# Two token-mixing items queued behind the last attention's products with v, and w_out converted beside the last channel mixing

## The chip, the cores and the metric

The kernel runs on one core of a Trainium2 chip. Its engines are called TensorE (PE in the rows, PEld for its weight loads), VectorE (DVE), ScalarE (ACT), GpSimd (POOL) and SyncE (SP, which here issues every DMA). The metric is the device time of one launch in microseconds; the time before is the median of three runs.

## What is computed

```python
def _attn_ref(q, k, v):                       # 4 batches, 8 heads, 576 tokens, 64 features a head
    scores = scale * q @ k^T                  # heads 0-3: a window of 32 keys; heads 4-7: every 4th of 128
    return softmax(masked scores) @ v
def _moe_ref(x, w_theta, w_tok_r, w_tok_i, w_ch):
    theta = x @ w_theta
    zr = x * cos(theta);  zi = x * sin(theta)
    u = x + w_tok_r @ zr + w_tok_i @ zi       # token mixing, over 576 tokens
    return u + max(u @ w_ch, 0)               # channel mixing, 512 x 512
def _moe2_ref(x, w_in, w_spatial, b_spatial, w_out):
    h = max(x @ w_in, 0);  u, v = halves of h # 512 features each
    v_n = layer norm of v
    return (u * (w_spatial @ v_n + b_spatial)) @ w_out
```

The three functions follow one another for each of four batches. All products are made in fp32 accuracy by splitting both operands into a high and a low part and adding three products (high-high, low-high, high-low). Some weights arrive as 64-bit floats and are converted on the chip.

## The kernel before, in words

**Attention** of batch b is 12 groups (four pairs of heads, three groups g each), numbered 12b to 12b+11. A group makes scores, then two steps later transposes, then two steps after that products with v (`att_values`; g = 0 makes none, g = 1 makes 24 products for it and g = 0, g = 2 makes 12). ScalarE copies the result ps_x to x. The last two groups of batch 3 are 46 and 47.

**Theta** (`th_unit`) takes 128 tokens: VectorE makes a high and a low part of x (xh, xl, two buffers each), TensorE makes 12 products ps_th and four transposes of x, ScalarE and VectorE make sine and cosine, and VectorE and GpSimd make z in two parts (zh, zl). A unit t covers tokens 128t to 128t+127; the last 64 tokens of batches 2 and 3 share one unit (`th_shared`), which needs both batches' x. `th_keep` saves batch 2's part of it in xs.

**Token mixing** (`tm_run`) has eight items for a batch: two halves of the tokens times four stripes of 128 features. With K_MAIN an item is 8 x 3 products that add up in one tile ps_y of PSUM; VectorE adds it to x. The ninth part, k = 8, comes from the shared theta unit and is mixed later as items of its own for batch 2, three products each, which also split x into uh and ul.

**Channel mixing** (`ch_run`) has eight items ps_r of 12 products; each result is split into `parts` and stored to x2d in DRAM.

**Weights for the second half** (w_in, w_sp, w_out) are converted by the 32 jobs of `second` and stored to DRAM from two buffers `parts`, which channel mixing of batches 0 to 2 uses too. A job of w_out loads 64-bit words into a tile w64 (four buffers), shifts them on ScalarE (L128) and VectorE (L131 to L133), rounds them to the high part on ScalarE (L107) and subtracts for the low part on GpSimd (L144). Staging tiles come from a tag `stage` with four buffers, which `w_half` also uses; `w_half` is the first thing beside the last channel mixing.

**The second half** runs in pairs of batches: `hv_unit` (five a pair's first batch, four the second's), `hu_run`, `sp_run` (spatial gating; its last operands are vhl and vhb) and `out_unit`, each with tiles from `ps_2`.

**Order.** `spread` traces a main generator and, at given rates, fills beside it. A planner then sets each engine's queue from a simulated timeline, in which an instruction that is ready may go ahead of earlier ones that are not; tiles of one tag are handed out in the order of the program. The queue of each engine is then fixed and in order. PSUM has eight banks: `ps_mm` four (attention's scores, theta, mixing), `ps_t` three, `ps_v` one (c64, the scratch of the conversion).

Of the kernel before, what the change touches and what calls it, by code (L numbers as in the profile page):

```python
# [11 lines left out]
F32 = mybir.dt.float32  # L12
# [6 lines left out]
PSUM = bass.MemoryType.PSUM  # L19
# [4 lines left out]
P = 128  # L24
# [4 lines left out]
T = 64  # L29
KW = T + WIN  # L30
NT = S // T
NA = 6
# [12 lines left out]
ATT_RATE, ATT_RATE_PAIR = 2.0, 3.0  # L45
TAIL_RATE = 1.0
CH_BEFORE = 4
PE_MASK = 1
PAIR = 2


IN_ENG, SP_ENG, OUT_ENG = "vgg", "ag", "aga"
# [5 lines left out]
K_MAIN = (0, 4, 1, 5, 2, 6, 3, 7)  # L58
# [4 lines left out]
def tile_block(ctx: ExitStack, tc: tile.TileContext, qT, kT, vw, eye_in, mask_in, eye_b_in, w_theta, w_tok, w_ch, w_in, w_sp, w_sph, b_sp, w_out, out):  # L63
    nc = tc.nc
    V, A, G, PE, SY = nc.vector, nc.scalar, nc.gpsimd, nc.tensor, nc.sync
# [6 lines left out]
    ps_mm = ctx.enter_context(tc.tile_pool(name="ps_mm", bufs=4, space=PSUM))  # L72
# [23 lines left out]
    wth_h = pth.tile([P, 4, DM], F32R, name="wth_h")  # L96
    wth_l = pth.tile([P, 4, DM], F32R, name="wth_l")
    patt = tc.alloc_tile_pool(name="patt", bufs=2, side="right")
    ps_t = tc.alloc_tile_pool(name="ps_t", bufs=3, space=PSUM)

    ps_v = tc.alloc_tile_pool(name="ps_v", bufs=1, space=PSUM)
    c64 = ps_v.tile([P, 512], F32, name="c64")


    def copy(dst, src, eng):
# [85 lines left out]
    groups = [(b, hp, g) for b in range(B) for hp in range(4) for g in range(3)]  # L191
    att = {}
    heads = {}

    def att_load(b, hp):
        early = b == 0 and hp >= 2
# [73 lines left out]
    def att_values(m):  # L270

        b, hp, g = groups[m]
        if g == 0:
            return
        qz, kt, vt, pT = heads[b, hp]
        ps = ps_t.tile([P, 512], F32, tag="pt", name="ps_x")
        if g == 1:
            for t in range(NA):
                for j in range(2):
                    PE.matmul(ps[T * j:T * (j + 1), T * t:T * (t + 1)], vt[:, t, T * j:T * (j + 1)], pT[j][:, T * t:T * (t + 1)], start=True, stop=True)  # L280
        else:
            for t in range(NB):
                for j in range(2):
                    PE.matmul(ps[T * j:T * (j + 1), T * t:T * (t + 1)], vt[:, NA + t, T * j:T * (j + 1)], pT[2][:, P * t + T * j:P * t + T * (j + 1)], start=True, stop=True)
        n0, n1 = (0, NA * T) if g == 1 else (NA * T, S)
        if hp < 2:
            A.copy(x[b][:, hp, n0:n1], ps[:, :n1 - n0])
            return

        xv = x[b][:, hp, :].rearrange("p (i r) -> p r i", r=4)  # L290
        if g == 1:
            A.copy(xv[:, :2, :], ps[:, :2 * SEQ].rearrange("p (r i) -> p r i", r=2))
            A.copy(xv[:, 2, :NA * T - 2 * SEQ], ps[:, 2 * SEQ:NA * T])
        else:
            A.copy(xv[:, 2, NA * T - 2 * SEQ:], ps[:, :3 * SEQ - NA * T])
            A.copy(xv[:, 3, :], ps[:, 3 * SEQ - NA * T:NB * T])

    def attention(b):

        n0, n1 = 12 * b, 12 * (b + 1)  # L300
        for m in range(n0, n1 + LAG_V):
            if n0 <= m - LAG_V < n1:
                att_values(m - LAG_V)
            if n0 <= m - LAG_T < n1:
                att_transpose(m - LAG_T)
            if m < n1:
                att_scores(m)
            yield
# [65 lines left out]
    def th_shared(b):  # L374
        th_unit(b, 4, True)
        yield

    def th_run(b, ts):
        for t in ts:
            th_unit(b, t)  # L380
            yield
# [58 lines left out]
    def run(gen):  # L440
        for _ in gen:
            pass

    def spread(main, *fills):

        acc = [0.0] * len(fills)
        for _ in main:
            for i, (gen, rate) in enumerate(fills):
                acc[i] += rate
                while acc[i] >= 1.0:  # L450
                    acc[i] -= 1.0
                    next(gen, None)
        for gen, _ in fills:
            run(gen)

    def jobs(fns):
        for f in fns:
            f()
            yield

    def take(gen, n):
        for _ in range(n):
            yield next(gen)

    def chain(*gens):
        for g in gens:
            yield from g
# [11 lines left out]
    second = jobs(j_in + j_sp + j_out)  # L479
# [9 lines left out]
    spread(th_run(0, (4, 0, 1, 2, 3)), (jobs([lambda f=f: behind(f) for f in j_tok0]), 2.0))  # L489
    for b in range(PAIR):  # L490
        ch = ch_run(b)
# [3 lines left out]


    th_keep(PAIR)
    spread(tm_run(PAIR, K_MAIN, False), (chain(attention(PAIR + 1), th_shared(PAIR)), ATT_RATE_PAIR), (take(second, 10), 1.25))
    spread(th_run(PAIR + 1, (0, 1, 2, 3)), (chain(tm_run(PAIR, (8,)), ch_run(PAIR)), TAIL_RATE), (second, 2.5))
    patt.release()  # L500
    ps_v.release()
    ps_t.release()
    pth.release()

# [58 lines left out]
    def w3():  # L563
        if w3_jobs:
            w3_jobs.pop(0)()

    for _ in ch_run(3):
        w3()
    p1.release()

    p2 = tc.alloc_tile_pool(name="p2", bufs=1, side="left", reuse_waits="tile")
    ps_2 = tc.alloc_tile_pool(name="ps_2", bufs=4, space=PSUM)

    wo_h = p2.tile([P, 4, DM], F32R, name="wo_h")
    wo_l = p2.tile([P, 4, DM], F32R, name="wo_l")
# [1 line left out]
        SY.dma_start(f32(t), f32(wo_d[:, :, i]))  # L577

    def mmtile(name):
        return ps_2.tile([P, 512], F32, tag="m2", name=name)  # L580

    vh, vl, vhl = {}, {}, {}
    hu = {}
# [126 lines left out]
    for pr in (0, 2):  # L710
# [20 lines left out]
        out_unit(b0, 4)  # L731
        out_unit(b1, 3, 2 if pr else 1)
    ps_2.release()
    p2.release()
    p2s.release()
    p2r.release()
# [59 lines left out]
```

## Time and profile before

| | |
|---|---|
| median of three runs (lowest to highest) | 570.19 us (569.38 to 571.11) |
| the profiled execution, its span | 569.31 us, 567.5 us |
| mean granted clock of TensorE | 0.982 |
| busy: TensorE, its weight loads | 534.8 us (94%), 478.4 us (84%) |
| busy: VectorE, ScalarE, GpSimd | 331.0 us (58%), 241.9 us (43%), 262.1 us (46%) |
| moved by DMA | 76.07 MB, 134 GB/s over the span |

The span is the time from the first to the last instruction of the profiled execution. Matmuls are pipelined: their durations overlap, so the pace is read from the distance of their starts. A granted clock of 1.00 is 2.4 GHz, 0.50 is 1.2 GHz. All positions in the rows are microseconds from the start of the span.

### The profile page before, as it was taken

The page shows a single profiled execution, that of the slowest core. Times are in us where ns is not written, and L with a number is a line of the kernel's source. Part 1 is how long each engine was busy: PE and PEld are TensorE (multiplying, and loading weights), DVE is VectorE, ACT ScalarE, POOL GpSimd, SP SyncE. Part 2 cuts the span into 40 slices and gives each one's busy share as a digit, 9 for nine tenths or more (in the row PEclk, how much of TensorE's full clock was granted, in tenths as well). Part 3 has the DMA queues.
Part 4 walks back from the last instruction along what each step waited for, and adds up shares of the span by engine and source line. Part 5 has one row for each costly group of instructions (what it writes and reads, how often), then busy time and mean ns, then how long its engine had stood idle before and what let it go on. Part 6 is the DMA issues. An engine that isn't in the chain of part 4 may idle for free.

```text
span 567.5 us, 11263 instructions
## 1 busy us (share of the span) xinstructions
PE 534.8 (94%) x4148; PEld 478.4 (84%) x4148; DVE 331.0 (58%) x844; ACT 241.9 (43%) x710; POOL 262.1 (46%) x333
## 2 busy tenths in 40 slices
PE   5887689999999999998899999999999999999997
PEld 3665578888988999877888999899899889988996
DVE  3589899898797269747697115773610327354030
ACT  3766476635655435766444212432322224223222
POOL 3484687552995348944349534334211203332040
PEclk9979799999999999999799999999999999999999
DMA  8845636672259453667400799705025110001002
GB/s 213 221 129 171 162 112 181 196 216 82 74 176 263 138 163 106 206 208 233 144 8 33 264 362 381 242 3 167 0 75 164 42 55 1 1 1 68 8 1 94
DMA packets 49935, 76.07 MB, mean 134 GB/s; under 512 B 4052, under 2 KB 30552, under 8 KB 49880
## 3 DMA queue, kind: packets, MB, share of 16 engines
q1 hardware_dynamic: 49880, 75.35, 43.3%
q8 instruction: 33, 0.54, 0.4%
q14 instruction: 22, 0.18, 0.1%
HBM read 52.53 MB, written 22.81 MB: 133 GB/s over the span
## 4 chain that ended last, share of the span: by engine, by line
PE 62%; DVE 10%; DMA 9%; POOL 7%; ACT 5%; issue 5%; SPq 1%; POOLq 0%; DVEq 0%; ACTq 0%
PE ps_y L411 12%; PE ps_sp L671 9%; PE ps_hu L652 9%; PE ps_o L700 9%; PE ps_hv L607 9%; PE ps_r L430 6%; POOL zl L316 2%; DMA wsp_d<-parts 2%; PE ps_th L341 2%; DMA w<-w_theta 1%; PE s L238 1%; DMA kt<-kT 1%; PE pt L266 1%; DVE xl L336 1%; DMA x2d<-parts 1%
## 5 line engine op out<-in xcount | busy, mean ns | idle before, releaser
L411 PE MATMUL ps_y<-wtok_h,zh 128*128 128x288 f32 x270 | 81.8, 306 | 1.7 <-DVE ta L346 0.9
L411 PE MATMUL ps_y<-wtok_h,zl 128*128 128x288 f32 x270 | 81.1, 301 | 0.4 <-POOL zl L316 0.4
L411 PE MATMUL ps_y<-wtok_l,zh 128*128 128x288 f32 x270 | 80.0, 298 | 0.0
L316 POOL TENSOR_TENSOR gl<-hu,gh 128x288 fp32r<-128x288 f32 x32 | 26.0, 811 | 74.6 <-ACT gh L107 74.6
L411 PEld LDWEIGHTS ps_y<-wtok_h,zh 128*128 128x128 f32 x270 | 50.7, 189 | 4.9 <-DVE sm L249 1.3
L675 DVE TENSOR_TENSOR hu<-ps_sp,hu 128x288 f32<-128x288 f32 x32 | 14.6, 455 | 66.8 <-PE ps_sp L674 66.8
L411 PEld LDWEIGHTS ps_y<-wtok_h,zl 128*128 128x128 f32 x270 | 51.0, 189 | 1.9 <-POOL zl L316 0.8
L411 PEld LDWEIGHTS ps_y<-wtok_l,zh 128*128 128x128 f32 x270 | 50.8, 189 | 0.2
L316 POOL TENSOR_TENSOR vl<-hv,vh 128x512 fp32r<-128x512 f32 x16 | 20.9, 1304 | 62.6 <-ACT vh L107 55.2
L256 POOL TENSOR_TENSOR sm<-sm,l 128x288 f32<-128x288 f32 x48 | 32.0, 673 | 31.6 <-DVE l L255 26.0
L253 ACT ACTIVATE sm<-sm,m 128x96 f32<-128x96 f32 x108 | 39.1, 364 | 13.4 <-DVE m L250 9.5
L316 POOL TENSOR_TENSOR ul<-x,uh 128x288 fp32r<-128x288 f32 x32 | 26.4, 832 | 25.2 <-ACT uh L107 25.1
L671 PE MATMUL ps_sp<-wsp_h,vh 128*128 128x288 f32 x128 | 37.8, 296 | 0.0
L430 PE MATMUL ps_r<-uh,wch_h 128*128 128x288 f32 x128 | 37.8, 296 | 0.0
L671 PE MATMUL ps_sp<-wsp_l,vh 128*128 128x288 f32 x128 | 37.8, 296 | 0.0
L671 PE MATMUL ps_sp<-wsp_h,vl 128*128 128x288 f32 x128 | 37.8, 295 | 0.0
L652 PE MATMUL ps_hu<-x2l,win_h 128*128 128x288 f32 x128 | 37.7, 295 | 0.0
L652 PE MATMUL ps_hu<-x2h,win_h 128*128 128x288 f32 x128 | 37.7, 295 | 0.0
L652 PE MATMUL ps_hu<-x2h,win_l 128*128 128x288 f32 x128 | 37.7, 295 | 0.0
L430 PE MATMUL ps_r<-uh,wch_l 128*128 128x288 f32 x128 | 37.7, 296 | 0.0
L316 POOL TENSOR_TENSOR parts<-x,parts 128x288 fp32r<-128x288 f32 x32 | 26.8, 844 | 23.4 <-ACT parts L107 23.4
L430 PE MATMUL ps_r<-ul,wch_h 128*128 128x288 f32 x128 | 37.4, 295 | 0.0
(169 smaller groups left out, 1590.9 us busy)
## 6 DMA issues: line engine op xcount, KB each, us to landing
x2d<-parts SPq DMA_DIRECT2D x32, 288.0 KB, 2.3
vt<-vw SPq DMA_DIRECT2D x16, 432.0 KB, 4.7
w<-w_tok SPq DMA_DIRECT2D x18, 288.0 KB, 2.8
x2h<-x2d SPq DMA_DIRECT2D x8, 576.0 KB, 7.7
x2l<-x2d SPq DMA_DIRECT2D x8, 576.0 KB, 10.9
kt<-kT SPq DMA_DIRECT2D x15, 304.0 KB, 4.5
w<-w_in SPq DMA_DIRECT2D x16, 256.0 KB, 3.5
win_d<-parts SPq DMA_DIRECT2D x16, 256.0 KB, 2.2
```

The costliest lines, as they stand in the source:

```text
L238: PE.matmul(o, qz[:, j, T * t:T * (t + 1)], kt[:, T * t:T * t + KW], start=not on_pe, stop=not on_pe)
L253: ia = A.activation(sm[:, t, :], src[:, t, :], AF.Exp, bias=m_[:, t:t + 1], scale=scale, accum_out=l[:, t:t + 1])
L256: ig = G.tensor_tensor(sm, sm, l.unsqueeze(2).to_broadcast([P, 3, KW]), op=ALU.mult)
L316: (G if el == "g" else V).tensor_tensor(dst_l, src, f32(dst_h), op=ALU.subtract)
L341: PE.matmul(ps, lh[:, k, :], rh[:, k, :], start=(i == 0), stop=(i == 11))
L411: PE.matmul(ps[:, :CH], lh[b, k][:, P * d:P * (d + 1)], rh[:, k, cs], start=(n == 0), stop=(n == 3 * len(ks) - 1))
L430: PE.matmul(ps[:, :CH], lh[:, k, P * e:P * (e + 1)], rh[:, k, cs], start=(n == 0), stop=(n == 11))
L607: PE.matmul(ps, lh[:, k, ts_], rh[:, k, DM:], start=(n == 0), stop=(n == 11))
L652: PE.matmul(ps[:, :CH], lh[:, k, fs], rh[:, k, cs], start=(n == 0), stop=(n == 11))
L671: PE.matmul(ps[:, :CH], lh[b, k][:, fs], rh[:, k, cs], start=(n == 0), stop=False)
L675: V.tensor_tensor(t[:, f, cs], ps[:, :CH], t[:, f, cs], op=ALU.mult)
L700: PE.matmul(ps, lh[:, k, ts_], rh[:, k, cs], start=(n == 0), stop=(n == 11))
```

## The change

Items 7 and 8 of batch 2's token mixing (`HELD` = 2) are taken out of the spread with batch 3's attention. They are traced after it, ahead of the shared theta unit, each inside `issue_after`, which queues its products behind the last product with v of group 46 and of group 47, as an order in TensorE's queue and not as a wait for their results. The shared theta unit is traced after them. Two of the last ten weight jobs (w_sp) stay beside batch 3's theta; the eight of w_out are traced one by one beside the eight items of the last channel mixing. Since c64 is then used later, `ps_v` is allocated below `ps_t` and kept to the end; `ps_2` has three banks instead of four, and the tiles of the second half alternate between it and the four of `ps_mm`.

```diff
+HELD = 2
...
-    ps_t = tc.alloc_tile_pool(name="ps_t", bufs=3, space=PSUM)
...
     c64 = ps_v.tile([P, 512], F32, name="c64")
+    ps_t = tc.alloc_tile_pool(name="ps_t", bufs=3, space=PSUM)
...
+    values = {}
...
-                    PE.matmul(ps[T * j:T * (j + 1), T * t:T * (t + 1)], vt[:, t, T * j:T * (j + 1)], pT[j][:, T * t:T * (t + 1)], start=True, stop=True)
+                    values[m] = PE.matmul(ps[T * j:T * (j + 1), T * t:T * (t + 1)], vt[:, t, T * j:T * (j + 1)], pT[j][:, T * t:T * (t + 1)], start=True, stop=True)
...
-    spread(tm_run(PAIR, K_MAIN, False), (chain(attention(PAIR + 1), th_shared(PAIR)), ATT_RATE_PAIR), (take(second, 10), 1.25))
-    spread(th_run(PAIR + 1, (0, 1, 2, 3)), (chain(tm_run(PAIR, (8,)), ch_run(PAIR)), TAIL_RATE), (second, 2.5))
+
+    tm = tm_run(PAIR, K_MAIN, False)
+    spread(take(tm, 8 - HELD), (attention(PAIR + 1), ATT_RATE_PAIR), (take(second, 10), 1.25))
+    for i in range(HELD):
+        with tc.issue_after(values[12 * (PAIR + 2) - HELD + i].ins):
+            next(tm)
+    run(tm)
+    run(th_shared(PAIR))
+    spread(th_run(PAIR + 1, (0, 1, 2, 3)), (chain(tm_run(PAIR, (8,)), ch_run(PAIR)), TAIL_RATE), (take(second, 2), 0.5))
     patt.release()
-    ps_v.release()
     ps_t.release()
...
     for _ in ch_run(3):
         w3()
+        next(second, None)
...
-    ps_2 = tc.alloc_tile_pool(name="ps_2", bufs=4, space=PSUM)
+    ps_2 = tc.alloc_tile_pool(name="ps_2", bufs=3, space=PSUM)
+    turn = [0]
...
     def mmtile(name):
-        return ps_2.tile([P, 512], F32, tag="m2", name=name)
+        turn[0] += 1
+        return (ps_2 if turn[0] % 2 else ps_mm).tile([P, 512], F32, tag=("mm", "m2")[turn[0] % 2], name=name)
...
     ps_2.release()
+    ps_v.release()
```

## Rows read from the trace of the kernel before

**Rows 1.** The page: TensorE's busy time, share of the span, instructions.
```profile
PE 534.8 (94%) x4148; PEld 478.4 (84%) x4148; DVE 331.0 (58%) x844; ACT 241.9 (43%) x710; POOL 262.1 (46%) x333
```

**Rows 2.** Windows: length, busy us (instructions) PE PEld DVE ACT POOL, clock, DMA share, GB/s.
```profile
265.00:270.00 5.00, 2.05 (x41) 1.49 (x39) 3.89 (x10) 2.44 (x8) 1.45 (x2) 0.88 0.73 227
270.00:275.00 5.00, 3.24 (x14) 3.18 (x15) 3.76 (x8) 2.64 (x9) 2.45 (x3) 0.50 0.37 128
```

**Rows 3.** Timeline of PE: start, us, instruction, count [idle before <-releaser].
```profile
265.97 0.92 PE L280 MATMUL ps_x<-pT,vt 96*64 96x64 f32 x24
268.20 0.57 PE L284 MATMUL ps_x<-pT,vt 96*64 96x64 f32 x12 [1.32 <-ACT pT L268]
271.76 1.08 PE L349 MATMUL ps_xn<-ident,xs 128*128 128x128 f32 x4 [2.98 <-DVE xs L329]
...
274.20 0.77 PE L341 MATMUL ps_th<-wth_h,xh 128*128 128x512 f32 x1
274.77 0.44 PE L411 MATMUL ps_y<-wtok_h,zh 128*128 128x288 f32 x1
...
280.24 0.40 PE L341 MATMUL ps_th<-wth_l,xh 128*128 128x512 f32 x1
280.47 0.29 PE L411 MATMUL ps_y<-wtok_h,zh 128*128 128x288 f32 x1
...
283.93 0.29 PE L411 MATMUL ps_y<-wtok_l,zh 128*128 128x288 f32 x1
```

**Rows 4.** Timeline of ACT: casts and copies at the hole, one cast later.
```profile
267.37 0.41 ACT L107 CAST parts<-w64g 128x256 fp32r<-128x256 f32 x1 [1.18 <-DMA wsp_d<-parts]
...
269.80 0.41 ACT L107 CAST parts<-w64g 128x256 fp32r<-128x256 f32 x1 [0.71 <-DMA wo_d<-parts]
270.11 0.66 ACT L292 COPY x<-ps_x 128x288 f32<-128x288 f32 x1
...
346.33 0.43 ACT L107 CAST parts<-x 128x288 fp32r<-128x288 f32 x1 [2.95 <-DMA x2d<-parts]
```

**Rows 5.** Windows: from the shared theta's end to channel mixing, and channel mixing.
```profile
280.60:300.90 20.30, 19.41 (x109) 16.59 (x107) 18.01 (x32) 11.12 (x20) 10.40 (x11) 1.00 0.07 21
300.90:313.60 12.70, 12.70 (x98) 12.70 (x97) 9.24 (x18) 5.73 (x12) 12.70 (x14) 1.00 0.14 48
```

**Rows 6.** Lines by form, whole span: count, busy us, mean ns, idle before, releasers.
```profile
L144 POOL TENSOR_TENSOR parts<-w64g,parts 128x256 fp32r<-128x256 f32 x24 | 18.0, 753 | 21.1 <-ACT parts L107 10.9 <-DVE parts L109 6.4 <-DVE l L254 2.6
L414 DVE TENSOR_TENSOR x<-ps_y,x 128x288 f32<-128x288 f32 x40 | 17.6, 449 | 33.1 <-PE ps_y L411 33.1
...
L131 DVE TENSOR_SCALAR c<-w 128x256 uint32<-128x256 uint32 x40 | 16.8, 421 | 3.1 <-DMA w<-w_theta 2.7
...
L128 ACT ACTIVATE w64g<-w 128x256 f32<-128x256 f32 x16 | 7.0, 438 | 7.0 <-DMA w<-w_ch 4.3 <-POOL parts L144 2.6
...
L107 ACT CAST parts<-w64g 128x256 fp32r<-128x256 f32 x8 | 3.2, 402 | 7.9 <-DMA wo_d<-parts 6.7 <-DMA wsp_d<-parts 1.2
```

**Rows 7.** Timeline of SP's queue: the fourth of four early loads of w_out.
```profile
221.56 0.34 SPq L121 DMA_DIRECT2D w<-w_out  x1
```

**Rows 8.** The chain of waits: start, us, what; the last channel mixing begins.
```profile
342.42 6.32 PE ps_r L430 x48
```

**Rows 9.** Windows: from the end of the last token mixing.
```profile
342.40:377.70 35.30, 35.30 (x226) 32.84 (x225) 25.12 (x66) 12.77 (x30) 13.40 (x14) 1.00 0.65 230
```

**Rows 10.** Timeline of DVE beside hv and hu of batch 0.
```profile
364.13 0.15 DVE L620 TENSOR_TENSOR r<-r 128x1 f32<-128x1 f32 x1
...
367.52 1.06 DVE L620 TENSOR_TENSOR r<-r 128x1 f32<-128x1 f32 x1
...
378.09 1.50 DVE L636 CAST vhb<-hs 64x512 fp32r<-64x512 f32 x1
```

**Rows 11.** Timeline of PE: the first read of vhb.
```profile
383.11 0.30 PE L674 MATMUL ps_sp<-wsp_lb,vhb 97*128 97x288 f32 x1
```

**Rows 12.** Timeline of POOL beside hv of batch 0.
```profile
367.26 1.30 POOL L316 TENSOR_TENSOR vl<-hv,vh 128x512 fp32r<-128x512 f32 x1 [1.01 <-ACT vh L107]
```

More of the change, by code (lines that the diff above doesn't have):

```diff
@@ L283, in att_values @@
                 for j in range(2):
-                    PE.matmul(ps[T * j:T * (j + 1), T * t:T * (t + 1)], vt[:, NA + t, T * j:T * (j + 1)], pT[2][:, P * t + T * j:P * t + T * (j + 1)], start=True, stop=True)
+                    values[m] = PE.matmul(ps[T * j:T * (j + 1), T * t:T * (t + 1)], vt[:, NA + t, T * j:T * (j + 1)], pT[2][:, P * t + T * j:P * t + T * (j + 1)], start=True, stop=True)
         n0, n1 = (0, NA * T) if g == 1 else (NA * T, S)
```

## The prediction

> **What bounds the kernel now.** I read the page first: TensorE is busy for 94% of a 567.5 us span [rows 1]. The reader is to see that little can be gained unless TensorE is idle or slow somewhere. The busy time in slices and the chain of waits showed where: after about 301 us it hardly stops, and before that its gaps are scattered. The largest, cut out with the windows, is at the end of the last attention: 2.05 us busy of 5, then 3.24 us of 5 at a granted clock of 0.50, which is the lower of its two levels, 1.2 GHz [rows 2]. TensorE's timeline shows the order inside it: the products with v of group 46, a gap of 1.32 us, those of group 47, a gap of 2.98 us, twelve transposes for theta and one theta product at half speed, and only then 21 products of mixing item 7, all of whose inputs had been there throughout [rows 3]. An item is a sum for one stripe of 128 features and half the tokens, 24 products at K_MAIN. The queue is in order, so item 7 stood behind transposes that waited. ScalarE's timeline says for what: its copies of ps_x stand behind casts of converted weights, one of which waited 1.18 us for a store of w_sp, another 0.71 us for a store of w_out; x was copied at 270.11 [rows 4].
>
> **The change, part by part.**
>
> *Two items into the hole.* Products in this stretch run at (283.93 - 280.47) / 26 = 0.133 us each at full clock [rows 3], so items 7 and 8 are 48 x 0.133 = 6.4 us. Item 7 is queued behind the values of group 46, item 8 behind those of 47. Behind item 8 come the shared theta's transposes, and nobody else waits for them. The idle time 1.32 + 2.98 = 4.3 us is filled. The stretch at half clock ran from 271.76 to 274.77, 3.0 us, and would be 1.5 us at full clock [rows 3]. Gross gain at the hole: 5.8 us. If values 47 come late, item 7's 3.2 us cover the 1.32 us gap, so the added queue order costs nothing unless they come over 1.9 us later than now.
>
> *What is late next.* The 6.4 us were filler later: item 8 lies between the shared theta and the next one. Once they are gone, VectorE may set the pace. New end of the shared theta: 265.97 + 0.9 (values 46) + 6.4 + 0.5 (values 47, most of its 0.57) + 0.4 (four transposes: a third of the 2.44 us from 271.76 to 274.20, at twice the clock) + 12 x 0.23 (280.24 to 280.47, one theta product) = 276.9, against 280.47 now: 3.6 us earlier. From there to the first product of channel mixing at 300.9 VectorE was busy 18.0 of 20.3 us [rows 5]. Without the two items' adds (2 x 0.45 [rows 6]) 17.1 us remain. If it then works without a break, channel mixing starts at 276.9 + 17.1 = 294.0, 6.9 us earlier; if the 2.3 us of idleness stay too, at 296.3, 4.6 us earlier. TensorE's own hole allows 5.8. So the bounds are 4.6 and 5.8, and I take 5.3, since part of VectorE's idleness there was waiting for TensorE. GpSimd is full in the 12.7 us that follow [rows 5], but its work is the residues of the same theta units and starts when VectorE delivers them, so I let it move along; from there TensorE runs without a gap and keeps what it has.
>
> *w_out moved.* Eight jobs leave 255 to 282 us, where they stood in front of the copies of x. That relief is in the 5.3 already: items 7 and 8 cover the wait whether or not ScalarE is freed. In the new place each job costs VectorE three operations of 0.42 us, ScalarE 0.44 + 0.40, GpSimd 0.75 [rows 6], so 8 x 1.26 = 10.1 us, 6.7 us and 6.0 us, and 16 DMAs of 256 KB on SP's queue. They are now behind the loads of w_sph, w_in, x2 and w_sp and ahead only of the load of wo, which nobody reads before the first output products, two stages on. Four of the eight loads were issued by 221.56, far ahead of their place [rows 7]; I expect that again. Conversions will not follow them so early: the staging tiles are shared with w_half, which comes first and waits for the end of the last token mixing.
>
> From the end of that mixing, 342.4 [rows 8], to 377.7 VectorE is busy 25.1 of 35.3 us, idle 10.2 us [rows 9]. The work that hides w_out is thus TensorE's channel mixing, hv and hu, and the cover is as large as the 10.1 us to hide, to the microsecond. Behind it is a second reserve: the last operand that spatial gating needs from VectorE for batch 0, vhb, is done at 378.09 + 1.50 = 379.6 [rows 10] and is read at 383.11 [rows 11], 3.5 us later. Everything moves forward together, so this slack stays. If the idle time takes all of w_out, the cost is 0; if it takes none, 10.1 - 3.5 = 6.6 us of TensorE waiting. Much of that idleness is a wait for ScalarE's square root or for TensorE, and operations of 0.42 us fit into about half of it: 10.1 - 5.1 - 3.5 = 1.5 us. ScalarE's queue adds a little: with two buffers of parts its casts wait for stores, as at 346.33, for 2.95 us [rows 4]; casts of w_out will wait there the same way, with the evacuation of hv behind them. I take 1.8 us.
>
> *PSUM.* c64 keeps its bank to the end, ps_2 has three, and the tiles of the second half alternate with the four of ps_mm: seven instead of four. TensorE has no idle time there now, so nothing is gained, and the longer queue of open tiles is what softens a late VectorE. The swapped order of the two pools costs nothing: no instruction is added.
>
> *Sum.* -5.3 + 1.8 = -3.5 us. The profiled execution took 569.31 us (span and 1.8 us around it), which gives 565.8; it lies 0.9 us below the median of the three runs, so on their scale it is 566.7. I forecast **566.2 us**.
>
> **The rivals.**
>
> *A: the gain is eaten by w_out in its new place.* VectorE's idleness takes little, TensorE waits 4 to 5 us at the first tiles of spatial gating, and the total is within 0.3% (1.7 us, about what this measurement can tell from no change): -5.3 + 4.5 gives 568.5, 569.4 on the runs' scale. For it: 10.1 us of work for 10.2 us of holes. Against it: the 3.5 us of slack and the seven banks. Chance 0.18.
>
> *B: slower, VectorE locked out by GpSimd beside hv.* At 367.52 the 128x1 product L620 took 1.06 us and ended at 368.58; GpSimd's vl ran from 367.26 for 1.30 us, to 368.56 [rows 10, 12]. The same instruction took 0.15 us at 364.13 [rows 10]. So a short operation can be held for a whole subtraction, and w_out brings eight more of 0.75 us: up to 6.0 us on VectorE. With 5.1 us of holes used and 3.5 us of slack the wait at spatial gating becomes 10.1 + 6.0 - 5.1 - 3.5 = 7.5 us, and a gap of that size would be followed by half clock as now at 270, another 1.5 [rows 3]: 9.0 - 5.3 = +3.7, or 573.0 (573.9 on the runs' scale). It decides once TensorE's waiting there passes 5.3 us. Against it: not every subtraction meets such an operation. Chance 0.17. The Trainium skill speaks for this one: SBUF — State Buffer, Who interferes with whom, says that a VectorE instruction with two SBUF inputs contends with a GpSimd instruction that reads SBUF, and that the loser waits for the whole instruction. The trace agrees in the pair above, 1.06 against 0.15 us. By that rule alone, with every subtraction meeting a victim, the time would be this rival's.
>
> *C: the conversion isn't moved.* Its operands are ready early, as the four loads show, and the planner may fill VectorE's and ScalarE's gaps near 260 to 300 with it again. Then nothing is paid after 342, and the dense 18.0 us of VectorE [rows 5] take a part of it: 569.31 - 5.3 + 0 to 3, so 564 to 567. Against it: the shared staging tiles. Chance 0.10.
>
> **How the numbers follow.** The forecast as worked out has 0.55, A 0.18, B 0.17, C 0.10. Faster by over 0.3%: 0.55 + 0.10 = 0.65; within: 0.18; slower: 0.17. Best case: 5.8 us gained and nothing paid, 563.5 (564.4); worst of the unknown costs without B: -4.6 + 6.6 = +2.0, 571.3 (572.2). The range 562.8 to 571.6 leaves out most of B and the rare case that VectorE's full 6.9 us come through with nothing paid. The likeliest case alone spans 563.5 to 568.
>
> **What the profile after would show.** Right: between the values of groups 46 and 47 and the theta transposes stand 48 mixing products without a gap over 0.5 us; the clock stays at 1.00 from 265 to 280; the first channel mixing product of batch 2 lies near 295.5 and the first of the last token mixing about 5 us before 313.6; w_out's casts are after the last token mixing; a gap of 1 to 3 us stands ahead of or among the first tiles of spatial gating. Wrong: the shared theta ends no earlier than 279, so that VectorE's chain did not move; or TensorE waits more than 5 us after 340; or its gaps appear between the theta units of batch 3 at the size of what was gained.

## The result, and the profile after

The change makes the kernel faster: 564.17 us median of four runs (562.76 to 566.89) against 570.65 us for the kernel before on the same chip (569.38 to 571.32); the ratio is 0.9895, with an interval of 0.9851 to 0.9938. The forecast was 566.2 us. The profiled execution took 563.47 us, with a span of 561.7 us and a mean granted clock of 0.990. In the new file each line stands one to eleven further down: L238 is L240, L280 is L282, L284 is L286, L341 is L343, L349 is L351, L411 is L413, L430 is L432, L107 is L108, L636 is L647, L674 is L685.

The page after, TensorE's line, answers to [rows 1]; the busy time fell by 1.9 us and the span by 5.8.

```profile
PE 532.9 (95%) x4148; PEld 476.1 (85%) x4148; DVE 326.7 (58%) x843; ACT 242.2 (43%) x711; POOL 261.8 (47%) x333
```

TensorE's timeline after, which answers to [rows 3]:

```profile
263.04 0.92 PE L282 MATMUL ps_x<-pT,vt 96*64 96x64 f32 x24
263.89 0.40 PE L413 MATMUL ps_y<-wtok_h,zh 128*128 128x288 f32 x1
...
265.82 0.57 PE L286 MATMUL ps_x<-pT,vt 96*64 96x64 f32 x12
...
273.75 0.39 PE L343 MATMUL ps_th<-wth_l,xh 128*128 128x512 f32 x1
...
277.06 1.03 PE L351 MATMUL ps_xn<-ident,x 128*128 128x128 f32 x8
280.41 0.40 PE L413 MATMUL ps_y<-wtok_h,zh 128*128 128x288 f32 x1 [2.31 <-ACT zh L108]
280.64 0.55 PE L343 MATMUL ps_th<-wth_h,xh 128*128 128x512 f32 x1
...
284.98 0.29 PE L413 MATMUL ps_y<-wtok_h,zh 128*128 128x288 f32 x1
...
295.04 0.34 PE L432 MATMUL ps_r<-uh,wch_h 128*128 128x288 f32 x1
```

The gaps of 1.32 and 2.98 us are gone: the products with v of group 46 are followed by mixing products, those of 47 too. But a new gap of 2.31 us stands between the theta units. The first product of an extra item (k = 8, the shared unit's share) is queued ahead of the next unit's twelve, and it waits for zh; the twelve products behind it then take 4.34 us (280.64 to 284.98) instead of 12 x 0.23 = 2.76, most of them at half clock. The last product of the shared theta is the one at 273.75; at 0.23 us a product the unit ends at 273.98.

The windows after, over the same stretch as [rows 2] and on to the theta units (columns as there):

```profile
265.00:270.00 5.00, 5.00 (x46) 4.77 (x45) 2.62 (x6) 0.51 (x2) 0.00 (x0) 1.00 0.01 3
270.00:275.00 5.00, 5.00 (x30) 4.26 (x28) 1.25 (x3) 0.81 (x2) 0.00 (x0) 1.00 0.00 0
275.00:280.00 5.00, 3.10 (x18) 2.43 (x16) 4.01 (x8) 2.67 (x4) 0.00 (x0) 1.00 0.00 0
280.00:285.00 5.00, 4.59 (x14) 3.65 (x15) 2.24 (x4) 1.56 (x3) 2.57 (x2) 0.66 0.00 0
```

TensorE was busy 5.29 of 10 us between 265 and 275 and is busy 10.00 now. VectorE, which was to set the pace, has become light: 10.12 us in these 20. Every cast of w_out has left this place; they now start at 351.33 to 368.84.

And w_out's new place, beside hv and hu: windows, then VectorE's last operands for spatial gating, then TensorE's first reads of them (these two answer to [rows 10, 11]).

```profile
350.00:355.00 5.00, 5.00 (x26) 4.25 (x26) 4.76 (x13) 3.34 (x9) 2.98 (x4) 1.00 0.82 259
355.00:360.00 5.00, 5.00 (x24) 4.14 (x23) 5.00 (x21) 3.55 (x9) 0.74 (x1) 1.00 0.78 251
360.00:365.00 5.00, 5.00 (x30) 4.40 (x29) 4.96 (x18) 3.47 (x10) 4.27 (x4) 1.00 0.35 121
365.00:370.00 5.00, 5.00 (x40) 5.00 (x39) 4.93 (x17) 2.95 (x9) 3.69 (x5) 1.00 0.44 146
```

```profile
373.69 1.51 DVE L647 CAST vhb<-hs 64x512 fp32r<-64x512 f32 x1
```

```profile
377.21 0.29 PE L684 MATMUL ps_sp<-wsp_hh,vhl 128*128 128x288 f32 x1
377.34 0.30 PE L685 MATMUL ps_sp<-wsp_lb,vhb 97*128 97x288 f32 x1
```

VectorE is full from 350 to 370, TensorE stays busy throughout, and vhb is ready 2.1 us before it is read (3.5 before). From the first product of the last channel mixing to the end of vhb's cast, in the kernel before and then after:

```profile
342.26:379.59 37.33, 37.33 (x241) 34.88 (x240) 26.96 (x68) 13.81 (x32) 15.06 (x16) 1.00 0.62 219
336.43:375.20 38.77, 38.77 (x251) 36.27 (x250) 33.17 (x91) 19.81 (x49) 21.26 (x24) 1.00 0.74 247
```

Counted from that product, vhb is 1.44 us later than before; its first read is not (40.85 us before, 40.91 after).

**Where the time came from.** Three stretches can be cut at the first ps_r product of batch 0 and of batch 2. The start is the time to the first, the middle lies between them, the rest runs from the second to the end of the span. Before: 118.19, 182.70 and 266.61 us. After: 116.14, 178.90 and 266.66 us. The marks are these, the first two of the kernel before; the fourth, at 295.04, is above:

```profile
118.19 0.40 PE L430 MATMUL ps_r<-uh,wch_h 128*128 128x288 f32 x1
300.89 0.33 PE L430 MATMUL ps_r<-uh,wch_h 128*128 128x288 f32 x1
116.14 0.40 PE L432 MATMUL ps_r<-uh,wch_h 128*128 128x288 f32 x1
```

TensorE's queue holds the same products in the same order in the start, so its 2.05 us are scatter: the kernel before, run again, had 122.32. The change's own part in this pair of profiles is at most the middle, 3.80 us; the second half neither gains nor loses. The middle can be cut once more, at the first product with v of group 46. From there to the mark, called the tail below, TensorE does the same 188 products in every kernel of this document. The tail took 34.92 us before (265.97 to 300.89; 33.78 when run again) and 32.00 after (263.04 to 295.04), a gain of 2.92 in this pair. The other 0.88 us lie ahead of it, where the two profiles of the kernel before differ by 1.60 (147.78 and 149.38).

### The profile page after: what moved, and what is told of

It is laid out like the page before. It is cut to its first block, busy times and chain, and to the rows that moved or that the text cites. A ratio compares the mean times of both kernels' runs of the same rounds, so it can differ in the third digit from the quotient of the medians.

```text
span 561.7 us, 11231 instructions
## 1 busy us (share of the span) xinstructions
PE 532.9 (95%) x4148; PEld 476.1 (85%) x4148; DVE 326.7 (58%) x843; ACT 242.2 (43%) x711; POOL 261.8 (47%) x333
## 4 chain that ended last, share of the span: by engine, by line
PE 70%; POOL 7%; DVE 7%; DMA 6%; ACT 4%; issue 4%; SPq 1%; POOLq 0%; DVEq 0%; ACTq 0%
PE ps_y L413 15%; PE ps_sp L682 9%; PE ps_hu L663 9%; PE ps_o L711 9%; PE ps_hv L618 9%; PE ps_r L432 6%; PE ps_th L343 4%; PE s L240 2%; POOL zl L318 2%; DMA wsp_d<-parts 2%; PE pt L268 2%; PE ps_x L282 2%; DMA qz_2wch_h<-qT 2%; DMA win_d<-parts 1%; DVE xl L338 1%
## 5 line engine op out<-in xcount | busy, mean ns | idle before, releaser
L413 PE MATMUL ps_y<-wtok_h,zh 128*128 128x288 f32 x270 | 81.6, 305 | 3.3 <-ACT zh L108 2.3
L413 PE MATMUL ps_y<-wtok_h,zl 128*128 128x288 f32 x270 | 80.8, 300 | 0.4 <-POOL zl L318 0.4
L413 PE MATMUL ps_y<-wtok_l,zh 128*128 128x288 f32 x270 | 79.8, 297 | 0.0
L413 PEld LDWEIGHTS ps_y<-wtok_h,zh 128*128 128x128 f32 x270 | 50.3, 188 | 6.4 <-ACT zh L108 2.5
L413 PEld LDWEIGHTS ps_y<-wtok_h,zl 128*128 128x128 f32 x270 | 50.7, 188 | 1.8 <-POOL zl L318 0.8
L413 PEld LDWEIGHTS ps_y<-wtok_l,zh 128*128 128x128 f32 x270 | 50.6, 188 | 0.2
L416 DVE TENSOR_TENSOR x<-ps_y,x 128x288 f32<-128x288 f32 x40 | 17.6, 448 | 36.9 <-PE ps_y L413 36.9
L432 PE MATMUL ps_r<-uh,wch_h 128*128 128x288 f32 x128 | 37.8, 296 | 0.0
L432 PE MATMUL ps_r<-uh,wch_l 128*128 128x288 f32 x128 | 37.7, 296 | 0.0
```

Source lines behind the costliest of these rows:

```text
L413: PE.matmul(ps[:, :CH], lh[b, k][:, P * d:P * (d + 1)], rh[:, k, cs], start=(n == 0), stop=(n == 3 * len(ks) - 1))
L416: V.tensor_tensor(xv, ps[:, :CH], xv, op=ALU.add)
L432: PE.matmul(ps[:, :CH], lh[:, k, P * e:P * (e + 1)], rh[:, k, cs], start=(n == 0), stop=(n == 11))
```

## The experiments

The table gathers all runs; start, middle, tail (a part of the middle) and rest are read from the one profiled execution, the ratio from all executions beside the kernel before on the same chip. e1 to e4, e5 to e9 and e10 to e13 each ran on a chip of their own, with 570.89, 570.85 and 569.50 us for the kernel before, so medians are to be compared inside such a group only. "Old" is w_out's place ahead of the theta units, "new" beside the last channel mixing.

| run | held items | w_out | start | middle | tail | rest | median us | ratio (interval) |
|---|---|---|---|---|---|---|---|---|
| before | no | old | 118.19 | 182.70 | 34.92 | 266.61 | 570.65 | 1 |
| after | yes | new | 116.14 | 178.90 | 32.00 | 266.66 | 564.17 | 0.9895 (0.9851 to 0.9938) |
| e1 | yes | old | 118.58 | 181.58 | 33.97 | 266.64 | 570.14 | 0.9986 (0.9961 to 1.0012) |
| e2 | no | new | 118.04 | 181.75 | 29.85 | 266.61 | 565.44 | 0.9887 (0.9852 to 0.9921) |
| e3 | yes, no queue order | new | 120.29 | 180.08 | 30.88 | 266.63 | 566.80 | 0.9920 (0.9887 to 0.9954) |
| e4 | no | old | 122.32 | 183.16 | 33.78 | 266.52 | 571.66 | 0.9999 (0.9973 to 1.0025) |
| e5 | yes | new | 120.42 | 177.59 | 30.18 | 267.59 | 566.07 | 0.9918 (0.9899 to 0.9936) |
| e7 | yes | new, VectorE's part doubled | 118.18 | 177.43 | 30.41 | 267.89 | 568.46 | 0.9969 (0.9936 to 1.0002) |
| e8 | no | old, 3 buffers | 119.53 | 190.55 | 32.66 | 266.62 | 576.96 | 1.0110 (1.0080 to 1.0141) |
| e9 | no | old, GpSimd for ScalarE | 118.44 | 182.10 | 32.09 | 266.66 | 570.18 | 0.9988 (0.9970 to 1.0006) |
| e10 | no | new; VectorE's part also in the old | 120.11 | 179.29 | 29.98 | 266.60 | 567.66 | 0.9968 (0.9945 to 0.9990) |
| e11 | no | new; stores' part also in the old | 120.35 | 181.81 | 35.12 | 266.84 | 569.60 | 1.0004 (0.9982 to 1.0027) |
| e12 | yes | as e7, three PSUM banks | 120.60 | 177.67 | 30.43 | 270.93 | 570.22 | 1.0009 (0.9980 to 1.0038) |
| e13 | yes | new, w_sp cast on VectorE | 116.61 | 182.08 | 32.01 | 266.61 | 567.15 | 0.9960 (0.9931 to 0.9989) |

The first theory is the prediction's: the held items fill the hole, and that is the gain. The rival is that the gain comes from what leaves ScalarE's, VectorE's and GpSimd's queues in the old place.

**e1, the held items alone.** After, with w_out in its old place and PSUM as before:

```diff
-    spread(th_run(PAIR + 1, (0, 1, 2, 3)), (chain(tm_run(PAIR, (8,)), ch_run(PAIR)), TAIL_RATE), (take(second, 2), 0.5))
+    spread(th_run(PAIR + 1, (0, 1, 2, 3)), (chain(tm_run(PAIR, (8,)), ch_run(PAIR)), TAIL_RATE), (second, 2.5))
...
-        next(second, None)
```

> Only the two held items; w_out is converted in its old place, the second half has its four banks as before. Theory 1 (the whole gain is the two items in the hole, w_out's move is free but brings nothing): within 1 us of the changed kernel, so 4 to 6 us below the kernel before; no gap over 0.5 us between the values of group 46 and theta's transposes, and the same new gap of about 2.3 us between the theta units. Theory 2 (taking w_out's casts out of ScalarE's queue is half of it): the gain is 2 to 3 us at most, x is copied as late as in the kernel before, about 3 us after the values, and VectorE's theta chain starts that much later than in the changed kernel.

Measured: 0.9986, within what can be told from no change. ScalarE's timeline, then TensorE's:

```profile
274.43 0.41 ACT L108 CAST parts<-w64g 128x256 fp32r<-128x256 f32 x1 [1.13 <-DMA wo_d<-parts]
...
278.14 0.41 ACT L108 CAST parts<-w64g 128x256 fp32r<-128x256 f32 x1 [2.66 <-DMA wo_d<-parts]
279.85 0.41 ACT L108 CAST parts<-w64g 128x256 fp32r<-128x256 f32 x1 [1.30 <-DVE stage L564]
280.16 0.69 ACT L347 ACTIVATE ta<-ps_th,magic 128x512 f32<-128x512 f32 x1
```

```profile
285.51 0.40 PE L413 MATMUL ps_y<-wtok_h,zh 128*128 128x288 f32 x1 [4.32 <-ACT zh L108]
```

The hole ahead of the transposes is filled, as in the changed kernel. But ScalarE's queue still holds the casts of w_out, which wait for stores to free one of two buffers (the profile puts the last wait shown down to VectorE's use of a staging tile instead); the shared unit's ta stands behind them and starts only at 280.16, zh follows, and TensorE stands still for 4.32 us. The hole has moved, not gone: the tail takes 33.97 us, for 34.92 and 33.78 in the two profiles of the kernel before.

**e2, w_out alone.** After, with batch 2's items and the shared unit traced as before:

```diff
-    tm = tm_run(PAIR, K_MAIN, False)
-    spread(take(tm, 8 - HELD), (attention(PAIR + 1), ATT_RATE_PAIR), (take(second, 10), 1.25))
-    for i in range(HELD):
-        with tc.issue_after(values[12 * (PAIR + 2) - HELD + i].ins):
-            next(tm)
-    run(tm)
-    run(th_shared(PAIR))
+    spread(tm_run(PAIR, K_MAIN, False), (chain(attention(PAIR + 1), th_shared(PAIR)), ATT_RATE_PAIR), (take(second, 10), 1.25))
```

> Only w_out's move, with its PSUM banks; mixing items 7 and 8 as before. Theory 1: the hole stays, since the items are still behind the shared theta's transposes in TensorE's queue: within 1.5 us of the kernel before. Theory 2: x is copied about 2 us earlier, the gap of 2.98 us before the transposes shrinks to under 1.5 us, half clock does not follow, and 2 to 4 us are gained. Rival B of the prediction (w_out costs TensorE something beside hv) would make it slower than before by 2 us or more.

Measured: 0.9887, no less than the whole change. Its profiled execution was the longest of its six (568.29 us). TensorE's two largest gaps in it:

```profile
255.86 0.84 PE L268 MATMUL pt<-ident,sm 128*96 128x128 f32 x3 [3.50 <-ACT x L289]
...
272.55 0.63 PE L351 MATMUL ps_xn<-ident,xs 128*128 128x128 f32 x4 [1.34 <-DVE xs L331]
```

The gap of 3.50 us is the old one near 254 (1.30 us in before's profile, 1.80 in e4), a cast of w_sp that waits for a store. Ahead of the transposes, where before waited 1.32 and 2.98 us, 1.34 us remain with no item held back. The tail, of which the two ends follow, is shorter than after's, 29.85 us for 32.00; the middle is longer (181.75) by what lies ahead of the tail, the gap of 3.50 us among it.

```profile
269.94 0.92 PE L282 MATMUL ps_x<-pT,vt 96*64 96x64 f32 x24
...
299.79 0.33 PE L432 MATMUL ps_r<-uh,wch_h 128*128 128x288 f32 x1
```

**e3, no order in the queue.** After, with the two items traced at their new place but free to go earlier:

```diff
-        with tc.issue_after(values[12 * (PAIR + 2) - HELD + i].ins):
-            next(tm)
+        next(tm)
```

> The changed kernel without the edges that queue items 7 and 8 behind the values; the items are still traced ahead of the shared theta. If the order of the PSUM tiles alone frees them (the tile of an item no longer comes after theta's): same time as the changed kernel within 1 us. If the edges matter: the planner fills the attention with the items as soon as their tiles are free, the gap before theta's transposes is back, 2.5 to 4 us wide, and the time is 3 to 5 us above the changed kernel.

Measured: 0.9920. The interval overlaps with the whole change's; what the explicit order adds to the time is not resolved. Its profile has no gap over 0.3 us between the values of group 46 and the theta transposes, and the same wait of 2.31 us after them, so the items reach this place by their place in the program alone.

**e4, before once more**, as a measure of the scatter:

> The kernel before, unchanged, for how far its own profile moves. The queues of before and after are the same up to batch 2's mixing, yet in the profile after the mixing of batch 0 ends 2.05 us earlier. If that is chance in the first 100 us: the ratio is 1.000 within 0.3%, and this profile's position of the channel mixing of batch 0 lies 1 us or more off that of the first profile. If it is the same to 0.3 us, the 2 us belong to the change.

Measured: 0.9999; its twelve executions lie between 568.0 and 573.91 us.

**e5, theta ahead of the extra item.** After, with the first theta unit queued ahead of the first k = 8 item:

```diff
+    run(th_run(PAIR + 1, (0,)))
-    spread(th_run(PAIR + 1, (0, 1, 2, 3)), (chain(tm_run(PAIR, (8,)), ch_run(PAIR)), TAIL_RATE), (take(second, 2), 0.5))
+    spread(th_run(PAIR + 1, (1, 2, 3)), (chain(tm_run(PAIR, (8,)), ch_run(PAIR)), TAIL_RATE), (take(second, 2), 0.75))
```

> After, with the first theta unit of batch 3 queued ahead of the first extra item of token block 8, so that TensorE no longer waits 2.31 us at 280.41 for that item's input while the theta unit is ready. If that gap costs time to the end: first ps_r product of batch 2 some 30 us behind the values of group 46 instead of 32.0, and a time 2 to 3 us under after's, 561.5. If VectorE's chain to ps_r sets the pace there whatever TensorE is given: 32 us again and 564.2. The run without the held items had 30.0 us between the same two products, which speaks for the first.

Measured: 0.9918. The gap of 2.31 us and the half clock are gone; what is left of TensorE's waits up to channel mixing is 0.58 and 0.90 us for x from VectorE. The tail is 30.18 us, as expected, but the time is not the 561.5 that was to follow. The middle is 1.3 us shorter than after's, but the rest is 0.9 us longer (0.71 us of it another wait for x, at 303.69), and the times show no gain over after. VectorE takes most of it back.

**e7, VectorE's part of w_out doubled in the new place.** After, with three more operations in each of the eight jobs:

```diff
+        for _ in range(3 if twice[0] else 0):
+            V.scalar_tensor_tensor(gi, gi, 0xFFFFFFFF, gi, op0=ALU.bitwise_and, op1=ALU.bitwise_or)
...
+        twice[0] = True
     for _ in ch_run(3):
```

> After, with three more VectorE operations of 128x256 in each of w_out's eight conversions in the new place, 24 in all or about 9.9 us more on VectorE beside the last channel mixing. It tests that the cover there is used up: VectorE was busy all of 350 to 372 and its last operand for spatial gating had 2.0 us of slack. If so, TensorE waits 9.9 - 2.0 = 7.9 us at the first tiles of spatial gating and the time is 571 to 573. If there is cover left that the traces do not show (other tiles that TensorE can take first), the wait stays under 3 us and the time under 568.

Measured: the rest grew by 1.2 us only. VectorE's vhb, then TensorE's waits:

```profile
382.52 1.50 DVE L652 CAST vhb<-hs 64x512 fp32r<-64x512 f32 x1
```

```profile
379.88 0.66 PE L687 MATMUL ps_sp<-wsp_h,vh 128*128 128x288 f32 x3 [0.39 <-ACT vh L108]
...
383.80 0.40 PE L689 MATMUL ps_sp<-wsp_hh,vhl 128*128 128x288 f32 x1 [0.23 <-POOL vhl L651]
```

vhb is 8.8 us later than in after (8.3 counted from the first product of the last channel mixing), yet TensorE waits 0.39 and 0.23 us: its queue now holds the main products of several tiles first and adds vhl's and vhb's products last (from 383.80 instead of 377.21). So beyond the 2.1 us of slack there is a second reserve, the order of products. The median of the times is higher than this profile (which is the shortest of ten executions, 565.3 to 573.47 us), so that up to some 4 us may be lost in a typical one; this is not settled.

**e12, the same on three banks of PSUM.**

```diff
-        turn[0] += 1
-        return (ps_2 if turn[0] % 2 else ps_mm).tile([P, 512], F32, tag=("mm", "m2")[turn[0] % 2], name=name)
+        return ps_2.tile([P, 512], F32, tag="m2", name=name)
```

> The run with 9.9 us more of VectorE work beside the last channel mixing, with the products of the second half on three PSUM banks instead of seven in turn. There vhl was 8.8 us later and TensorE waited only 1.3 us more, for it took the main products of other tiles first and added vhl's last. If the seven banks made that possible, three hold up TensorE by 4 to 8 us at the first tiles of spatial gating, 570 to 574, and from the first ps_r product of batch 2 to the end it takes 271 us or more instead of 267.9. If three banks do as well, 268 us and the same time as the run before within 0.5%.

Measured: the rest is 270.93 us, 3.0 us more than with seven banks. TensorE's waits:

```profile
386.00 0.40 PE L688 MATMUL ps_sp<-wsp_hh,vhl 128*128 128x288 f32 x1 [0.46 <-POOL vhl L650]
...
388.55 0.40 PE L686 MATMUL ps_sp<-wsp_h,vh 128*128 128x288 f32 x1 [1.33 <-DVE hu L690]
```

With three open tiles TensorE does not run ahead of vhl as far as it did, and at 388.55 it waits for VectorE to empty one. Two more waits, of 0.50 and 0.35 us at 368.39 and 370.60, are among hu's products, for ScalarE to empty a tile. The banks are the reserve that the prediction named ("the longer queue of open tiles is what softens a late VectorE"), and they are worth 3.0 us in this pair of profiles, once VectorE is this late; the two ratios, 0.9969 and 1.0009, have intervals that overlap. That they matter in the changed kernel, whose VectorE is earlier, was not tried.

**e8, three buffers for the stores.** Before, with one buffer taken from the loads; channel mixing of batches 0 to 2 shares the third one:

```diff
-        st = const.tile([P, 2 * CH], U32, tag="w64", name="w64", bufs=4)
+        st = const.tile([P, 2 * CH], U32, tag="w64", name="w64", bufs=3)
...
-        t = const.tile([P, 2, CH], F32R, tag="parts", name="parts", bufs=2)[:, :, :n]
+        t = const.tile([P, 2, CH], F32R, tag="parts", name="parts", bufs=3)[:, :, :n]
...
-                pool, n_ = (const, 2) if b < B - 1 else (p2s, 8)
+                pool, n_ = (const, 3) if b < B - 1 else (p2s, 8)
```

> Before, with three buffers instead of two for the converted weights on their way to the store, and three instead of four for the loads; the work of w_out stays in its old place. If it is the waiting for stores in ScalarE's queue that costs, most of the gain comes without any move: 34.9 us between the values of group 46 and the first ps_r product of batch 2 become 30 to 32, and the time is 566 to 567.5. If it is the amount of work in that place (10 us on VectorE, 6.7 us on ScalarE), the stretch stays near 34 to 35 us and the time within 1 us of 570.6.

Measured: 1.1% slower, and the question stays open. The wait ahead of the transposes is down to 1.05 us, but TensorE lost far more elsewhere in the middle, 190.55 us long: from 230 to 240 it was busy 7.69 of 10 us (9.90 in before), and at 276.01 it had stood still for 3.99 us. ScalarE's waits from 225 to 282 (us in total, times, longest), in the kernel before and then two of e8:

```profile
ACT parts L107 <- DMA wo_d<-parts: 6.7, 4, 3.2
ACT w64g L128 <- DMA w<-w_out: 2.5, 3, 1.3
ACT parts L107 <- DMA wo_d<-parts: 0.4, 2, 0.2
```

The waits for w_out's stores are nearly gone. In their place ScalarE waits for w_out's loads, which it does not in before. Whether the store buffer would have paid without the lost load buffer was not tried.

**e9, ScalarE's part on GpSimd.** Before, with

```diff
-IN_ENG, SP_ENG, OUT_ENG = "vgg", "ag", "aga"
+IN_ENG, SP_ENG, OUT_ENG = "vgg", "ag", "ggg"
```

> Before, with w_out's scaling and rounding on GpSimd instead of ScalarE; place, VectorE's three operations per job and both buffers stay. If ScalarE's queue was what the copies of x and theta's inputs stood in, the stretch from values of group 46 to the first ps_r product of batch 2 falls from 34.9 us to 30 to 32 and the time to 566 to 568, unless GpSimd, which gets 16 more operations of some 0.75 us, becomes the limit and takes it back. If VectorE's 10 us in that place are what costs, the stretch stays at 34 to 35 us and the time at 570 or above.

Measured: 0.9988. The two gaps ahead of the transposes shrank to one and the tail to 32.09 us, but TensorE waited elsewhere:

```profile
255.51 0.85 PE L266 MATMUL pt<-ident,sm 128*96 128x128 f32 x3 [2.52 <-ACT x L287]
...
271.27 0.63 PE L349 MATMUL ps_xn<-ident,xs 128*128 128x128 f32 x4 [1.55 <-DVE xs L329]
...
286.44 0.40 PE L411 MATMUL ps_y<-wtok_h,zh 128*128 128x288 f32 x1 [1.81 <-ACT zh L107]
```

The first of these is the gap near 254, for a cast of w_sp, which the edit leaves alone and which lies between 0.74 and 3.50 us over the profiles; the last is new. By the times, freeing ScalarE alone brings nothing while the stores and the other engines' work stay there.

**e10 and e11, half of the work put back.** e2, and in w_out's old place eight jobs more whose results nobody reads. In e10 each is the load, GpSimd's scaling and VectorE's three operations, without a store; in e11 it is the load, ScalarE's scaling and cast, GpSimd's subtraction and the store, without VectorE.

```diff
+    again = jobs([lambda k=k, c=c: bits_job(k, c) for k in range(4) for c in range(2)])
-    spread(th_run(PAIR + 1, (0, 1, 2, 3)), (chain(tm_run(PAIR, (8,)), ch_run(PAIR)), TAIL_RATE), (take(second, 2), 0.5))
+    spread(th_run(PAIR + 1, (0, 1, 2, 3)), (chain(tm_run(PAIR, (8,)), ch_run(PAIR)), TAIL_RATE), (chain(take(second, 2), again), 2.5))
```

The job is e10's; e11 has its own in the same place.

> The kernel with w_out moved and no held items (ratio 0.9887), and in w_out's old place once more the load, GpSimd's scaling and VectorE's three integer operations of each of the eight jobs, with no cast, no residue and no store: about 10 us of VectorE there, nothing on ScalarE. If it is VectorE's work in the old place that cost, the gain is lost: 569 to 571. If it is what ScalarE, GpSimd's subtractions and the stores did, it stays at 565 to 566.

> The same kernel, and in w_out's old place once more the load, ScalarE's scaling and cast, GpSimd's subtraction and the store of each of the eight jobs, into a buffer that nobody reads: no VectorE. If ScalarE's queue and its waits for stores are what cost, 569 to 571. If only the two halves together cost (each fits where the other is away), both this and the run with VectorE's half stay under 567.5.

Measured: e11 loses the whole gain, 1.0004. ScalarE's casts and TensorE's gaps in e11:

```profile
268.40 0.41 ACT L511 CAST parts<-w64g 128x256 fp32r<-128x256 f32 x1 [1.07 <-DMA wsp_d<-parts]
...
270.54 0.40 ACT L511 CAST parts<-w64g 128x256 fp32r<-128x256 f32 x1 [0.42 <-DMA wo_x<-parts]
270.85 0.66 ACT L294 COPY x<-ps_x 128x288 f32<-128x288 f32 x1
...
276.50 0.40 ACT L511 CAST parts<-w64g 128x256 fp32r<-128x256 f32 x1 [1.87 <-DMA wo_x<-parts]
278.69 0.41 ACT L511 CAST parts<-w64g 128x256 fp32r<-128x256 f32 x1 [1.79 <-DMA wo_x<-parts]
280.64 0.41 ACT L511 CAST parts<-w64g 128x256 fp32r<-128x256 f32 x1 [1.55 <-DMA wo_x<-parts]
281.61 0.69 ACT L347 ACTIVATE ta<-ps_th,magic 128x512 f32<-128x512 f32 x1 [0.56 <-PE ps_th L343]
```

```profile
269.23 0.57 PE L286 MATMUL ps_x<-pT,vt 96*64 96x64 f32 x12 [1.28 <-ACT pT L270]
272.50 1.08 PE L351 MATMUL ps_xn<-ident,xs 128*128 128x128 f32 x4 [2.70 <-DVE xs L331]
```

These are before's two gaps again, 1.28 and 2.70 us for 1.32 and 2.98 [rows 3], with the same casts ahead of the copy of x as in [rows 4]. VectorE's work isn't needed for them, and the tail is as long as before, 35.12 us. e10 lies in between, 0.9968, and its profile shows nothing in this place that e2's doesn't: 1.35 us ahead of the transposes, a tail of 29.98 us for e2's 29.85, and a middle of 179.29 us, close to after's. So VectorE's half costs nothing in the tail. By the ratios it costs something, but e2 was not run on the same chip, and the profile doesn't show where. Which of ScalarE's work, GpSimd's subtractions and the stores does the harm is not told apart by e11, which puts back all three; that it is the casts waiting for stores is read from ScalarE's rows.

**e13, w_sp's cast on VectorE.** After, with `SP_ENG = "vg"` for `"ag"`:

> After, with the cast of w_sp (eight jobs at 245 to 258 us) on VectorE instead of ScalarE. In every profile TensorE waits 0.7 to 3.5 us near 251 to 258 for a copy of x on ScalarE that stands behind a cast of w_sp, which waits for a store. If the wait goes with the cast: that gap under 0.5 us and a time 1 to 2 us under after's, 562.5 to 563. If VectorE, which then waits for the same stores with the scores' maxima behind it, takes the gap over: the same time within 0.3%, or slower.

Measured: 0.9960, no better than after. VectorE, then TensorE:

```profile
251.40 0.31 DVE L110 CAST parts<-stage 128x288 fp32r<-128x288 f32 x1 [3.35 <-DMA wsp_d<-parts]
```

```profile
253.38 0.53 PE L268 MATMUL pt<-ident,sm 128*96 128x128 f32 x3 [3.13 <-POOL sm L258]
```

The wait for the store moved to VectorE and took the softmax with it; after's gap there was 0.98 us. On either engine, what is queued behind the waiting cast pays.

## Why the prediction was right, and where it was not

The time and its sign came out as forecast, and the sum is near: -3.5 us forecast; -3.80 in the pair of profiles once the start's scatter is taken out, and -6.5 between the medians, whose interval reaches from -3.5 to -8.5. Of the reasons about half held, and the sum is near partly by luck: the hole gave less than was forecast and w_out cost less, and the two misses cancel in part. The windows after, from the end of the shared theta to the first ps_r product, belong to the second point:

```profile
274.00:295.04 21.04, 18.58 (x92) 15.42 (x91) 15.64 (x30) 10.81 (x19) 9.76 (x10) 0.92 0.00 0
```

- **The hole was read rightly.** The two items lie where they were to lie, no gap over 0.5 us is left there, and the granted clock is 1.00 from 265 to 280. From the first product with v of group 46 to the end of the shared theta the sum gave 10.9 us; measured are 10.94 (263.04 to 273.98), for 14.50 before. The first ps_r product came at 295.04 for a forecast of 295.5, 2.05 us of it by a lucky start.
- **The gain at the hole, taken at 5.3 with bounds of 4.6 and 5.8, was 2.92,** the tail's, under its lower bound. The bounds assumed that behind the shared theta VectorE would set the pace, for 17.1 to 19.4 us to the first ps_r product. That stretch took 21.06 us (20.42 before), and VectorE was busy for 15.64 of them. What set the pace instead was TensorE's own queue, with a product waiting for zh ahead of twelve that were ready. That is the 2.31 us at 280.41, and the half clock behind it adds 4.34 - 2.76 = 1.58 us. The half clock is not fixed by the change: e7 and e12 have after's queues up to there, had full clock behind the same wait, and took 30.41 and 30.43 us for the tail, 4.5 less than before and 3.4 less than e4. Gaps between the theta units stood among the signs of being wrong.
- **The step that failed is the one that says whose gain it is:** "That relief is in the 5.3 already: items 7 and 8 cover the wait whether or not ScalarE is freed." e1 shows that they don't. They cover the first wait, and the casts that remain on ScalarE make the next, 4.32 us, out of the same stores. e2 shows the other side: with w_out gone, the times gain as much with no item held. e11 shows that the casts, subtractions and stores of w_out alone bring back the gaps and the whole time. That the held items add anything on top of w_out's move is not shown: by the ratios nothing (0.9895 with, 0.9887 without). In the tail the kernels with both take 30.18 to 32.01 us, those of e2 and e10 without held items 29.85 and 29.98. Their middles are no shorter for it (181.75 and 179.29, against 177.4 to 180.1 with both, e13 with its longer wait aside), since they waited 3.50 and 2.21 us for the cast of w_sp ahead of the tail, a wait that scatters.
- **w_out in its new place, taken at 1.8 with bounds of 0 and 6.6, costs nothing:** the rest is 266.66 us after and 266.61 before. The description was right, VectorE full and the slack down from 3.5 to 2.1 us, but the wait that was to follow did not come. The term that was too large is the 10.1 us, a sum of durations. VectorE's durations overlap where operations follow closely, and its busy time up to vhb grew by 33.17 - 26.96 = 6.21 us only. Its idle time took 4.77 of these (10.37 before, 5.60 after; the estimate had 5.1) and the slack the other 1.44. ScalarE's casts of w_out, which were to wait for stores, waited 0.15 us in all for them. A second reserve was not needed here: in e7, with 9.9 us more by durations, the reads of vhb move back behind other products, and the rest grows by 1.2 us in its one profile.
- **PSUM** costs nothing in the changed kernel, as forecast; whether it gives something there was not tried. e12 shows its banks as the reserve behind the last point.
- **Rival A** (TensorE waits 4 to 5 us at spatial gating) and **rival C** (the casts of w_out stay early) did not come: TensorE is busy throughout, and the casts lie from 351.33 to 368.84. **Rival B's** lock occurred and cost nothing: the 128x1 product, L631 after, took 0.93 us at 367.71 beside vl (367.32, 1.31 us), against 0.15 us free [rows 10]. It was held once in the five units of batch 0, for three times in the kernel before. The trace thus agrees again with the rule of the Trainium skill (SBUF — State Buffer, Who interferes with whom) that the prediction weighed; it bears on VectorE's time, which was not what TensorE waited for.

Open are the part that VectorE's work in the old place has in the loss (e10), whether another store buffer would have done instead of the move (e8), and whether the held items add anything.

## What to carry to other kernels

A wait read off the busiest engine is often a queue problem on another: look at what is queued ahead of the late copy, and ask whether it waits for a store. Filling the hole leaves that queue as it is, and here the wait came back at the next thing behind it. Taking the waiting instructions to another place in the program removed it (e2); taking them to another engine did not pay (e9, e13). Price added work by what the engine's busy time will grow, not by a sum of durations that overlap. And before pricing a late operand by its first read, see whether the reader has open tiles with which it can go ahead.

## What was not expected of the hardware

- **The start scatters by 6 us.** The first ps_r product of batch 0 came between 116.14 and 122.32 us over fourteen profiles, at 118.19 and 122.32 in two of the same kernel. A single pair of spans can't show a gain of 4 us. The middle scatters less: 182.70 and 183.16 for the kernel before, 178.90, 177.43 and 177.67 for three kernels whose queues are the same up to its end.
- **The same gap doesn't always bring half clock.** The wait of 2.31 us for zh is in after, e3, e7, e12 and e13, with the same products behind it. In after and e13 the granted clock of the 4.7 us that follow is 0.64, and TensorE gets 14 products done; in e3, e7 and e12 it stays at 1.00, with 25. In these three TensorE came to the wait from twelve theta products and eight transposes, as in after; what tells the cases apart does not show in the profiles.
